# Where the early dense products are summed: in the stage that makes them, or later from DRAM

## The chip, the cores and the metric

The kernel runs on one core of a Trainium2 chip. The metric is device microseconds (us) of one execution of the whole program; a version's time is the median of its runs. The engines are TensorE (PE; PEld is its weight load), VectorE (DVE), ScalarE (ACT), GpSimd (POOL) and SyncE (SP). Here SP issues nearly all loads from DRAM, POOL issues nearly all stores.

## The reference

The output mixes two branches on x (2048 tokens, 640 columns), all float32: an FNet mixing y and a dense layer with Mish, weighted by a gate per token.

```python
g = sigmoid((x * gate_w).sum(-1, keepdims=True))
a = x @ wd_re.T ; b = x @ wd_im.T          # 640 x 640
y = c_re @ a - c_im @ b                    # 2048 x 2048
h = x @ w1 + b1                            # 640 -> 1728
act = h * tanh(softplus(h))                # Mish
out = g * y + (1 - g) * (act @ w2)         # 1728 -> 640
```

The kernel computes the same by first mixing over the sequence (u), then over the hidden columns (y).

## The kernel before, in words

Each float32 operand is split into a high and a low part (ACT copies the high part, DVE subtracts for the low part), and each product is three matmuls of 128x512: high by high, high by low, low by high (`mm3`). Products are arranged in a Strassen-like scheme of sums and differences of blocks, whose partial results leave PSUM into SBUF, return into a bank, or wait in DRAM. A tile `f` is a 128x512 buffer in SBUF (18 of them, pool `FS`), `x` a 128x640 buffer (6, pool `X`), `w` and `r` are split operands, `ps` are the 8 banks of PSUM.

The program is not issued as it is written. Every operation is first recorded in a graph (`Graph.add`). The order of the matmuls is the order in which the program writes them. For the other engines a planner (`Graph.run`) goes through the program with a cost for each operation: it gives each a wish time (`want`), sorts what is ready by it, hands out buffers of a pool only if enough are free for those that asked before (`granted`), and holds an operation back until its `since`; `by` pulls a wish time forward. What comes out is one fixed list of instructions for each engine. On the chip each engine takes its own list strictly in order and waits where an input or a buffer isn't ready.

The stages in order: products with the sequence matrices c_im and c_re (problems `sq`, tiles of x as weights, matrices c streamed from DRAM), wd's products (`hd`), the dense products of the later token groups (`dense_first`), and w2's products with the output (`ou`). A part of the dense products stands at the very front: for token groups t of 0 and 1 and the first six blocks f of w1, `early_first` makes the products of two of the five 128-column parts of x and stores them in DRAM as `early` (12 tiles, read again much later by `dense_first`, which the change leaves alone), and `early_second` makes those of the other three. Their steps (`unit`, three of each, in two `lines`) are spread between the steps of the first stage's problems 2, 3 and 0, so that their matmuls stand between those of c.

In `early_second` a step that has a result calls `end(c, t, f)`: it loads the `early` tile, DVE adds the new result to it (from PSUM in nine of twelve calls, `tt` at L314, and from SBUF in the other three), and `out_act` has ACT make the Mish (L624), and POOL store it as `act` (L306). Between two products in one bank the step also saves the bank to SBUF (`to_sbuf`, `f<-ps` at L323) and puts a saved value back into it (`copy`, `ps<-f`, L323), and the next matmul into that bank waits for this copy. The planner's order on ACT therefore decides how soon PE can go on.

Of the kernel before, what the change touches and what calls it, by code (L numbers as in the profile page):

```python
# [15 lines left out]
P = 128  # L16
# [11 lines left out]
DELAY, RATE = 2.2, 370e3  # L28
CALM, CALM_DMA, NEAR = 1.0, 3.0, 3.0
GATES = 130.0, 10.0  # L30
GATED = 600.0, 7.0


# [16 lines left out]
class Graph:  # L50
# [75 lines left out]
    def run(self, pools):  # L126

        self.wants()
        for op in self.ops:
            for v in op.vals:  # L130
                if v.pool and (v.ask is None or op.want < v.ask[0]):
                    v.ask = op.want, op.n, id(v)
        for op in self.ops:
            for v in op.vals:
                if v.pool and v.ask[1] == op.n:
                    also = [u.ask[0] for u in op.vals if u.pool is v.pool and u is not v]
                    if also:
                        v.ask = min(v.ask, (max(also), op.n, id(v)))
        for p in pools:
            p.asks = sorted({v.ask for op in self.ops for v in op.vals if v.pool is p})  # L140
            p.soon = sorted({v.ask for op in self.ops if op.prompt for v in op.vals if v.pool is p and v.ask[1] == op.n})
        missing = {op.n: len(op.deps) for op in self.ops}
        free = {e: 0.0 for e in ("PE", "ACT", "DVE", "SP", "POOL")}
        ready = {e: [] for e in free}
        pe = [op.n for op in self.ops if op.engine == "PE"][::-1]
        for op in self.ops:
            if not missing[op.n]:
                insort(ready[op.engine], (op.want, op.n))
        events, now, left, dma = [], 0.0, len(self.ops), 0.0
        waits = sorted({op.since for op in self.ops})  # L150

        def granted(op, blocked):
            for v in op.vals:
                if v.pool and v.t is None:
                    if v.pool in blocked:
                        return False
                    p, n = v.pool, bisect_left(v.pool.asks, v.ask)
                    if not op.prompt:
                        n += bisect_left(p.soon, (v.ask[0] + AHEAD,)) - bisect_left(p.soon, v.ask)
                    if len(p.free) <= n:  # L160
                        blocked.add(v.pool)
                        return False
            return True

        def bequeath(p):
            if p.heir and not p.asks:
                p.heir.free += [p.part(t) for t in p.free]
                p.free = []

        while left:  # L170
            began = False
            for e, line in ready.items():
                if free[e] > now + 1e-9 or not line:
                    continue
                if e == "PE":
                    i = next((i for i, x in enumerate(line) if x[1] == pe[-1]), None)
                    if i is not None and not granted(self.ops[pe[-1]], set()):
                        i = None
                else:
                    blocked = set()  # L180
                    i = next((i for i, x in enumerate(line)
                              if self.ops[x[1]].since <= now and granted(self.ops[x[1]], blocked)), None)
                if i is None:
                    continue
                op = self.ops[line.pop(i)[1]]
                if e == "PE":
                    pe.pop()
                for v in op.vals:
                    if v.pool and v.t is None:
                        v.pool.asks.remove(v.ask)  # L190
                        if v.ask in v.pool.soon:
                            v.pool.soon.remove(v.ask)
                        v.t = v.pool.free.pop(0)
                        bequeath(v.pool)
                op.emit()
                free[e] = now + op.hold
                if e in ("SP", "POOL"):
                    dma = max(now + DELAY, dma) + op.moves
                    end = dma + 0.1
                else:  # L200
                    end = now + op.took + 0.03
                heapq.heappush(events, (end, op.n, False))
                left -= 1
                began = True
            if began:
                continue
            times = [t for e, t in free.items() if t > now + 1e-9 and ready[e]]
            times += [t for t in waits if t > now][:1]
            if events:
                times.append(events[0][0])  # L210
            assert times, ("stuck", left, pe and self.ops[pe[-1]].at, [(p.name, len(p.free)) for p in pools])
            now = max(now, min(times))
            while events and events[0][0] <= now + 1e-9:
                _, n, held = heapq.heappop(events)
                op = self.ops[n]
                if held:
                    insort(ready[op.engine], (op.want, op.n))
                    continue
                for v in op.vals:
                    v.left -= 1  # L220
                    if not v.left and v.pool:
                        p = v.pool
                        p.free.append(v.t)
                        bequeath(p)
                for a in op.after:
                    missing[a.n] -= 1
                    if not missing[a.n]:
                        wait = min(CALM_DMA if op.engine in ("SP", "POOL") else CALM, a.want - now - NEAR)
                        if a.engine in ("ACT", "DVE") and wait > 0:
                            heapq.heappush(events, (now + wait, a.n, True))  # L230
                        else:
                            insort(ready[a.engine], (a.want, a.n))
# [8 lines left out]
def fnet_mish_gate(ctx: ExitStack, tc: tile.TileContext, xn, xt, c_re, c_im, wd_re, wd_im,  # L241
# [21 lines left out]
    def dram(name, rows=P, cols=N):  # L263
        return Val(t=dr.tile([rows, cols], F32, name=name))
# [33 lines left out]
        op.by, op.since = by, since  # L298
        return v

    def load_of(pool, d, rows=P):
        return load(pool, lambda: d.t, d, rows)

    def store(d, v, rows=P, queue=None):
        queue = queue or STORES
# [313 lines left out]
    def raw(t, k):  # L619
        return load(FS, xt[t, k])  # L620
# [80 lines left out]
        out_act(FC, t, a, a, FR, False)  # L701

    H = FP // 2
    early = {(t, f): dram(f"early{t}_{f}") for t in range(2) for f in range(FP)}

    def w1_twice(k0, fifth=False):

# [69 lines left out]
    def early_second():  # L777

        at, x = w1_twice(2, True), x_twice(2)
        d = [operand(raw(t, KD - 1), W) for t in range(2)]  # L780

        def unit(j):
            a, b = bank(), bank()

            def end(c, t, f):
                o = load_of(FS, early[t, f])
                tt(o, c, o, OP.add)
                out_act(f, t, o, o)
            mm3(a, at["b11", j], x["a11"], True, True)
            p = to_sbuf(a)  # L790
            yield
            mm3(b, at["t1", j], x["s1"], True, True)
            yield
            mm3(a, at["b21", j], x["a12"], False, False)
            mm3(a, at[("d", 0), j], d[0], False, True)
            end(a, 0, j)
            copy(a, p)
            yield
            mm3(a, at["t2", j], x["s2"], False, True)
            u = to_sbuf(a)  # L800
            yield
            mm3(a, at["t3", j], x["s3"], False, True)
            v = to_sbuf(a)
            tt(v, b, v, OP.add)
            yield
            mm3(b, at["b22", j], x["s4"], False, False)
            mm3(b, at[("d", 1), j], d[0], False, True)
            tt(u, b, u, OP.add)
            end(u, 0, j + H)
            yield  # L810
            mm3(a, at["t4", j], x["a22"], False, False)
            mm3(a, at[("d", 0), j], d[1], False, True)
            end(a, 1, j)
            yield
            copy(b, v)
            mm3(b, at[("d", 1), j], d[1], False, True)
            end(b, 1, j + H)
            yield
        kept.update(x, d=d)
        return [unit(j) for j in range(H)]  # L820
# [3 lines left out]
    def early_rests():  # L824
        for t, ks in ((0, ("a11", "a12")), (1, ("a21", "a22"))):
            dense_rest(t, [operand(raw(t, k)) for k in range(2)] + [kept[k] for k in ks] + [kept["d"][t]])

    def dense_first(tp):
        t1, t2 = tp, tp + 2
# [156 lines left out]
    for q in range(4):  # L986
        sq[q].second(seq.low)
        if q == 2:
            gates()
        sq[q].third()  # L990
    hd[0].first(hid.top)
    hd[1].first(hid.top)
    for p in hd:
# [58 lines left out]
```

## Time and profile before

| what | value |
|---|---|
| time, median of 3 runs (lowest, highest) | 865.77 us (864.66, 866.73) |
| profiled execution, whole | 866.31 us |
| its span, first to last instruction | 864.5 us |
| PE busy | 856.1 us, 3754 matmuls |
| DVE, ACT, POOL busy | 694.5, 486.9, 91.8 us |
| mean granted TensorE clock | 0.998 |
| moved by the DMA engines | 220.27 MB |

The span is 1.8 us shorter than the profiled execution's time; the rest lies around it. PE is busy in 99% of the span, so a time of this kernel is the number of matmuls by the distance of their starts, plus whatever time PE stands still or runs at a lower clock. Where PE has no gap, no other engine's work costs anything.

### The profile page before, as it was taken

Reading aid. Unit: us, or ns where it says so; the run is one execution under the profiler, and the core shown is the slowest. Engines: PE = TensorE matmul, PEld = TensorE weight load, DVE = VectorE, ACT = ScalarE, POOL = GpSimd, SP = SyncE. Lnnn points to the kernel's source line nnn. Section 1 sums busy time; section 2 is a strip of 40 time slices with the busy share of each in tenths; the row PEclk is TensorE's granted clock in tenths of the full one; section 3 lists DMA queues with packets and bytes.
Section 4 is the critical chain, followed back from the end, with each engine's and each line's share of the span. In section 5 each row is a group of like instructions: output and inputs, shape, how many; then the busy total and the mean of one; then the engine's idle time right before and its main releaser. Section 6 shows DMA issues by size and latency. Waiting matters only on the chain.

```text
span 864.5 us, 12193 instructions
## 1 busy us (share of the span) xinstructions
PE 856.1 (99%) x3754; PEld 704.8 (82%) x3754; DVE 694.5 (80%) x1241; ACT 486.9 (56%) x902; POOL 91.8 (11%) x167
## 2 busy tenths in 40 slices
PE   8999999999999999999999999999999999999998
PEld 6887788888888888888888888888888888888886
DVE  7978789986896778677999978997787996758493
ACT  6976776535354654456576733676566764533242
POOL 0122110002000200100020001022222100004000
PEclk9999999999999999999999999999999999999999
DMA  9888786777885957395778839678798876637943
GB/s 331 303 321 303 258 284 235 258 250 268 306 278 177 357 178 233 129 346 194 233 239 314 298 111 368 228 249 304 272 306 314 314 257 239 197 117 170 367 163 122
DMA packets 110946, 220.27 MB, mean 255 GB/s; under 512 B 13920, under 2 KB 18144, under 8 KB 110880
## 3 DMA queue, kind: packets, MB, share of 16 engines
q1 hardware_dynamic: 97184, 177.14, 60.0%
q0 software_dynamic: 13552, 42.22, 13.9%
q8 instruction: 29, 0.48, 0.2%
q14 instruction: 37, 0.30, 0.1%
q10 hardware_dynamic: 144, 0.13, 0.0%
HBM read 174.59 MB, written 44.84 MB: 254 GB/s over the span
## 4 chain that ended last, share of the span: by engine, by line
PE 97%; DMA 2%; DVE 0%; ACT 0%; issue 0%; SPq 0%; ACTq 0%; DVEq 0%
PE ps L350 97%; DMA x<-in_xn_dram 1%; DMA x<-in_w1a_dram 1%; DMA f<-in_c_im_dram 1%; SPq L296 0%; DVE f L314 0%; DVE x L314 0%; DVE r1l L345 0%; DVE r4l L345 0%; ACT r1h L344 0%; ACT ps L323 0%; ACT w19h L335 0%; ACT f L323 0%; DVE f L601 0%; ACT f L599 0%
## 5 line engine op out<-in xcount | busy, mean ns | idle before, releaser
L314 DVE TENSOR_TENSOR f<-f,f 128x512 f32<-128x512 f32 (+1 forms) x322 | 214.2, 683 | 5.1 <-DMA f<-act 2.0
L323 ACT ACTIVATE f<-ps 128x512 f32<-128x512 f32 x149 | 87.1, 595 | 63.4 <-PE ps L350 58.0
L314 DVE TENSOR_TENSOR f<-ps,f 128x512 f32<-128x512 f32 x101 | 66.9, 685 | 44.2 <-PE ps L350 34.2
L306 POOL DMA_DIRECT2D u<-f x40 | 21.6, 541 | 303.2 <-DVE f L314 289.8
L344 ACT ACTIVATE r9h<-f 128x512 fp32r<-128x512 f32 x40 | 25.3, 631 | 29.0 <-PE ps L350 20.5
L306 POOL DMA_DIRECT2D act<-f x52 | 28.1, 541 | 116.8 <-ACT f L624 74.1
L344 ACT ACTIVATE r5h<-f 128x512 fp32r<-128x512 f32 x38 | 24.0, 631 | 28.0 <-PE ps L350 22.2
L314 DVE TENSOR_TENSOR x<-x,x 128x256 f32<-128x256 f32 (+2 forms) x88 | 38.0, 445 | 2.2 <-DMA x<-in_xn_dram 1.5
L344 ACT ACTIVATE r1h<-f 128x512 fp32r<-128x512 f32 x39 | 24.5, 629 | 25.1 <-PE ps L350 19.6
L344 ACT ACTIVATE r4h<-f 128x512 fp32r<-128x512 f32 x38 | 23.9, 630 | 24.3 <-PE ps L350 18.7
L323 ACT ACTIVATE ps<-f 128x512 f32<-128x512 f32 x56 | 33.0, 598 | 8.2 <-DVE f L314 7.8
L344 ACT ACTIVATE r0h<-f 128x512 fp32r<-128x512 f32 x38 | 23.9, 629 | 23.8 <-PE ps L350 14.2
L344 ACT ACTIVATE r6h<-f 128x512 fp32r<-128x512 f32 x38 | 24.0, 631 | 23.2 <-PE ps L350 14.6
L344 ACT ACTIVATE r2h<-f 128x512 fp32r<-128x512 f32 x38 | 23.9, 629 | 22.8 <-PE ps L350 16.6
L344 ACT ACTIVATE r7h<-f 128x512 fp32r<-128x512 f32 x38 | 24.0, 631 | 21.5 <-PE ps L350 11.9
L345 DVE TENSOR_TENSOR r9l<-f,r9h 128x512 fp32r<-128x512 f32 x40 | 27.5, 686 | 10.5 <-ACT r9h L344 10.3
L344 ACT ACTIVATE r3h<-f 128x512 fp32r<-128x512 f32 x39 | 24.5, 628 | 19.9 <-PE ps L350 14.0
L344 ACT ACTIVATE r8h<-f 128x512 fp32r<-128x512 f32 x36 | 22.7, 630 | 21.2 <-PE ps L350 10.9
L345 DVE TENSOR_TENSOR r6l<-f,r6h 128x512 fp32r<-128x512 f32 x38 | 26.1, 686 | 10.4 <-ACT r6h L344 10.2
L345 DVE TENSOR_TENSOR r1l<-f,r1h 128x512 fp32r<-128x512 f32 x39 | 26.7, 686 | 9.0 <-ACT r1h L344 8.6
L624 ACT ACTIVATE f<-f,b1s 128x512 f32<-128x512 f32 x36 | 25.9, 718 | 14.1 <-DVE f L314 13.8
L345 DVE TENSOR_TENSOR r2l<-f,r2h 128x512 fp32r<-128x512 f32 x38 | 26.1, 688 | 9.5 <-ACT r2h L344 8.9
(2185 smaller groups left out, 2696.2 us busy)
## 6 DMA issues: line engine op xcount, KB each, us to landing
f<-in_c_im_dram SPq DMA_DIRECT2D x128, 256.0 KB, 4.7
f<-in_c_re_dram SPq DMA_DIRECT2D x128, 256.0 KB, 4.2
f<-act SPq DMA_DIRECT2D x84, 256.0 KB, 4.6
f<-u SPq DMA_DIRECT2D x80, 256.0 KB, 4.1
act<-f POOLq DMA_DIRECT2D x52, 256.0 KB, 4.0
f<-in_xt_dram SPq DMA_DIRECT2D x42, 256.0 KB, 4.3
u<-f POOLq DMA_DIRECT2D x40, 256.0 KB, 4.2
x<-in_xn_dram SPq DMA_DIRECT2D x24, 320.0 KB, 4.8
```

The lines of the kernel that those rows point to most:

```text
L306: dma(queue, lambda: ISSUE[queue].dma_start(d.t, v.t[:rows]), whole(v), whole(d), rows * N * 4)
L314: dve(lambda: nc.vector.tensor_tensor(o.t[rows, x], a.t[rows, y], b.t[rows, z], op=op), whole(a, b), whole(o), n)
L323: act(lambda: nc.scalar.activation(o.t, a.t, AF.Copy, scale=scale), whole(a), whole(o))
L344: act(lambda: nc.scalar.activation(r.t[0][:, :N], src.t[:, :N], AF.Copy), whole(src), [(r, 0)])
L345: dve(lambda: nc.vector.tensor_tensor(r.t[1][:, :N], src.t[:, :N], f32(r.t[0][:, :N]), op=OP.subtract), whole(src) + [(r, 0)], [(r, 1)])
L350: G.add("PE", lambda: nc.tensor.matmul(bank.t, w.t[wn][:, k * P:k * P + P], x.t[xn_][:, :N], start, stop, skip_group_check=True), [(w, (k, ...
L624: act(lambda: nc.scalar.activation(o.t[rows], src.t[rows], AF.Mish, **more), whole(src, table) + whole(b1s) * bias, whole(o), more=0.1)
```

## The change

`early_second` no longer loads the `early` tiles. Its twelve results are copied out of PSUM by ACT where they are in a bank (nine of them; three are already in SBUF) and stored by POOL in new DRAM tiles `late`. A new function `early_acts` loads each `early` tile with its `late` tile, adds the two on DVE, and then makes the Mish and the store as before. Its twelve sums are to begin, by the planner's clock, at 300 us and every 8 us after it. The planner also gets a second rule (`tight`) for the case that nothing can begin and no event is pending; then a result in PSUM may take a buffer that an earlier asker was waiting for.

```diff
+SUMS = 300.0, 8.0
...
                     p, n = v.pool, bisect_left(v.pool.asks, v.ask)
+                    if op.prompt and tight:
+                        n = bisect_left(p.soon, v.ask)
                     if not op.prompt:
...
+            if not times and not tight:
+                tight = True
+                continue
...
-            def end(c, t, f):
-                o = load_of(FS, early[t, f])
-                tt(o, c, o, OP.add)
-                out_act(f, t, o, o)
+            def end(o, t, f):
+                store(late[t, f], o)
...
-            end(a, 0, j)
+            end(to_sbuf(a), 0, j)
...
             end(u, 0, j + H)
...
-            end(a, 1, j)
+            end(to_sbuf(a), 1, j)
...
-            end(b, 1, j + H)
+            end(to_sbuf(b), 1, j + H)
...
+    def early_acts():
+
+        for i, key in enumerate(early):
+            since = SUMS[0] + SUMS[1] * i
+            o, v = (load_of(FS, d[key], since=since) for d in (early, late))
+            tt(o, o, v, OP.add)
+            G.ops[-1].by = since + SUMS[1]
+            out_act(key[1], key[0], o, o)
...
         sq[q].third()
+    early_acts()
     hd[0].first(hid.top)
```

The list of matmuls keeps its order (other buffers aside); the lists of the other engines move nearly everywhere, since the planner's choices follow from each other.

Place 1 is ACT's list in the second half of the early dense stage. The names: `w..h<-x` are high parts of weights from loads, `r..h<-f` high parts of streamed operands from loads, `f<-ps` is a save of a bank, `ps<-f` a value put back, `f<-f,b1s` a Mish. Before, from one value put back (`ps_70`) to the next (`ps_67`):

```order
L323 ACTIVATE ps_70<-f_100 128x512
L624 ACTIVATE f_109<-f_109,b1s 128x512
L335 ACTIVATE w2h<-x_115 128x256
L335 ACTIVATE w16h<-x_115 128x128
L323 ACTIVATE f_100<-ps_70 128x512
L344 ACTIVATE r2h<-f_96 128x512
L335 ACTIVATE w15h<-x_112 128x640
L344 ACTIVATE r0h<-f_99 128x512
L335 ACTIVATE w19h<-x_113 128x640
L323 ACTIVATE ps_67<-f_95 128x512
```

And now, between the same two:

```order
L331 ACTIVATE ps_70<-f_100 128x512
L343 ACTIVATE w18h<-x_112 128x128
L352 ACTIVATE r9h<-f_104 128x512
L331 ACTIVATE f_102<-ps_70 128x512
L343 ACTIVATE w17h<-x_116 128x640
L343 ACTIVATE w21h<-x_111 128x640
L331 ACTIVATE f_100<-ps_67 128x512
L331 ACTIVATE ps_67<-f_93 128x512
L352 ACTIVATE r7h<-f_103 128x512
L331 ACTIVATE f_109<-ps_70 128x512
L352 ACTIVATE r0h<-f_110 128x512
```

The Mish is gone, a save of `ps_67` has come in ahead of its return, and the two copies `r7h` and `r0h` from loads, one of which stood ahead of the value put back, stand behind it.

Place 2 is SP's list of loads at the same place. Before:

```order
L296 DMA f_96<-in_c_re_dram 128x512
L296 DMA f_103<-early_4_300 128x512
L296 DMA f_99<-in_xt_dram 128x512
L296 DMA x_113<-in_w1a_dram 128x640
L296 DMA f_106<-early_2_298 128x512
L296 DMA x_111<-in_xn_dram 128x640
L296 DMA f_93<-in_xt_dram 128x512
L296 DMA f_96<-early_5_295 128x512
L296 DMA f_109<-in_xt_dram 128x512
```

And now:

```order
L304 DMA f_104<-in_xt_dram 128x512
L304 DMA f_108<-in_c_re_dram 128x512
L304 DMA f_98<-in_c_re_dram 128x512
L304 DMA f_96<-in_c_re_dram 128x512
L304 DMA f_103<-in_xt_dram 128x512
L304 DMA f_97<-in_c_re_dram 128x512
L304 DMA f_110<-in_xt_dram 128x512
L304 DMA x_112<-in_w1b_dram 128x320
L304 DMA x_115<-in_xn_dram 128x512
L304 DMA x_116<-in_xn_dram 128x640
L304 DMA x_111<-in_w1a_dram 128x640
```

Before, the two x tiles (`in_xt`) and the block of w1 (`in_w1a`) for the copies of place 1 stood between loads of `early`; now no load of `early` is there, and the x tiles stand four to ten rows ahead of the block of w1.

Place 3 is SP's list in the course of the last two problems of the first stage. Before:

```order
L296 DMA f_110<-in_c_re_dram 128x512
L296 DMA f_96<-in_c_im_dram 128x512
L296 DMA f_100<-in_c_im_dram 128x512
L296 DMA f_101<-in_c_im_dram 128x512
L296 DMA f_97<-ps_319 128x512
```

And now:

```order
L304 DMA f_98<-in_c_im_dram 128x512
L304 DMA f_106<-in_c_im_dram 128x512
L304 DMA f_97<-early_0_296 128x512
L304 DMA f_102<-late_0_308 128x512
L304 DMA f_103<-ps_331 128x512
```

Two loads of one sum have come in between the streamed ones; eleven more such pairs stand in this part of the list, all of them ahead of the first load of `in_wd_im`.

More of the change, by code (lines that the diff above doesn't have):

```diff
@@ L168, in bequeath @@
                 p.free = []
+        tight = False
         while left:
@@ L205, in run @@
             if began:
+                tight = False
                 continue
@@ L299, in load, with load_of @@
         return v
-    def load_of(pool, d, rows=P):
-        return load(pool, lambda: d.t, d, rows)
+    def load_of(pool, d, rows=P, since=0.0):
+        return load(pool, lambda: d.t, d, rows, since=since)
     def store(d, v, rows=P, queue=None):
@@ L703, in fnet_mish_gate @@
     H = FP // 2
-    early = {(t, f): dram(f"early{t}_{f}") for t in range(2) for f in range(FP)}
+    early, late = ({(t, f): dram(f"{n}{t}_{f}") for t in range(2) for f in range(FP)} for n in ("early", "late"))
     def w1_twice(k0, fifth=False):
```

## The prediction

> **What bounds the kernel now.** First the head and the busy times of the page:
>
> ```profile
> span 864.5 us, 12193 instructions
> PE 856.1 (99%) x3754; PEld 704.8 (82%) x3754; DVE 694.5 (80%) x1241; ACT 486.9 (56%) x902; POOL 91.8 (11%) x167
> ```
>
> PE is the bound. The change adds no matmul and takes none away, so only time in which PE stands still or runs below its clock can be won or lost. The view of waits, asked for PE alone, has one row that matters (the others lie in the first 8 us, where the loads change by one swapped pair):
>
> ```profile
> PE ps L350 <- ACT ps L323: 2.4, 2, 1.9
> ```
>
> Two waits, both for a value that ACT puts back into a bank. PE's own timeline shows where they are, and what they cost (start, duration, ..., idle before and its releaser):
>
> ```profile
> 85.12 0.39 PE L350 MATMUL ps<-r0h,w1l 128*128 128x512 f32 x1
> 86.03 0.50 PE L350 MATMUL ps<-r6h,w25h 128*128 128x512 f32 x1 [0.52 <-ACT ps L323]
> ...
> 86.60 0.40 PE L350 MATMUL ps<-r6h,w25l 128*128 128x512 f32 x1
> ...
> 88.68 0.39 PE L350 MATMUL ps<-r8h,w2l 128*128 128x512 f32 x1
> ...
> 90.72 0.39 PE L350 MATMUL ps<-r1h,w25l 128*128 128x512 f32 x1
> 92.96 0.50 PE L350 MATMUL ps<-r6h,w25h 128*128 128x512 f32 x1 [1.85 <-ACT ps L323]
> ...
> 94.25 0.63 PE L350 MATMUL ps<-r7l,w3h 128*128 128x512 f32 x1
> ...
> 96.38 0.63 PE L350 MATMUL ps<-r7h,w3h 128*128 128x512 f32 x1
> ...
> 97.42 0.39 PE L350 MATMUL ps<-r5h,w22h 128*128 128x512 f32 x1
> ```
>
> The undisturbed step is read between the two holes: 88.68 to 90.72 is 9 steps, 2.04 / 9 = 0.2267 us. Hole 1, 85.12 to 86.60, is 3 steps: 1.48 - 0.68 = 0.80 lost. From 86.60 to 90.72 are 18 steps: 4.12 - 4.08 = 0.04. Hole 2, 90.72 to 97.42, is 13 steps: 6.70 - 2.95 = 3.75. Only about 2.0 of that is standing still; behind it the steps are 0.43 (94.25 to 96.38, 5 steps in 2.13), nearly double. The granted clock says why (window: length, busy times and counts of PE, PEld, DVE, ACT, POOL, then clock, DMA share, GB/s):
>
> ```profile
> 85.35:86.03 0.68, 0.16 (x1) 0.00 (x0) 0.68 (x3) 0.65 (x2) 0.00 (x0) 1.00 0.92 349
> 90.95:92.96 2.01, 0.16 (x1) 0.00 (x0) 1.46 (x3) 1.80 (x4) 0.00 (x0) 1.00 1.03 405
> 92.96:97.42 4.46, 4.46 (x12) 3.51 (x13) 3.21 (x7) 2.82 (x5) 0.54 (x1) 0.62 0.76 285
> ```
>
> After the hole of 2.01 us the mean clock was 0.62; the hole of 0.68 had no such sequel. The holes together cost 0.80 + 0.04 + 3.75 = 4.59 us.
>
> Why ACT was late, in ACT's timeline, and for hole 1 in DVE's:
>
> ```profile
> 85.38 0.60 ACT L323 ACTIVATE ps<-f 128x512 f32<-128x512 f32 x1 [2.08 <-DVE f L314]
> ...
> 90.84 0.63 ACT L344 ACTIVATE r0h<-f 128x512 fp32r<-128x512 f32 x1 [1.48 <-DMA f<-in_xt_dram]
> 91.68 0.74 ACT L335 ACTIVATE w19h<-x 128x640 fp32r<-128x640 f32 x1 [0.21 <-DMA x<-in_w1a_dram]
> 92.33 0.58 ACT L323 ACTIVATE ps<-f 128x512 f32<-128x512 f32 x1
> ```
>
> ```profile
> 83.11 0.42 DVE L314 TENSOR_TENSOR x<-x,x 128x256 f32<-128x256 f32 x1 [1.48 <-DMA x<-in_xn_dram]
> ...
> 84.66 0.68 DVE L314 TENSOR_TENSOR f<-ps,f 128x512 f32<-128x512 f32 x1
> ```
>
> Hole 1: DVE waited 1.48 for a load, so the sum in `end`, which must read the bank (84.66), was late, and ACT could not overwrite that bank before. Hole 2: ACT took its list in order, stood behind the late copy of an x tile (`r0h`, 1.48) and of a block of w1 (0.21), and reached the value for PE only at 92.33. Both come from loads that land late. SP's waits from 60 to 110 us and the landing times from 60 to 100 us say why these are late:
>
> ```profile
> SPq L296 <- DMA act<-f: 8.0, 4, 3.1
> SPq L296 <- DMA ps<-f: 6.3, 3, 5.4
> SPq L296 <- DMA early<-f: 4.3, 2, 2.6
> ```
>
> ```profile
> f<-early SPq DMA_DIRECT2D x7, 256.0 KB, 5.0
> ...
> ps<-f POOLq DMA_DIRECT2D x3, 256.0 KB, 7.0
> ...
> x<-in_w1a_dram SPq DMA_DIRECT2D x1, 320.0 KB, 5.3
> ```
>
> SP stands 18.6 us in these three rows for stores to land, since only then is an `f` buffer free for its next load; all later loads stand behind it. The `early` loads are seven of those that ask for such buffers here.
>
> **The change, part by part.** The durations come from the page's groups:
>
> ```profile
> L314 DVE TENSOR_TENSOR f<-f,f 128x512 f32<-128x512 f32 (+1 forms) x322 | 214.2, 683 | 5.1 <-DMA f<-act 2.0
> L323 ACT ACTIVATE f<-ps 128x512 f32<-128x512 f32 x149 | 87.1, 595 | 63.4 <-PE ps L350 58.0
> ...
> L306 POOL DMA_DIRECT2D act<-f x52 | 28.1, 541 | 116.8 <-ACT f L624 74.1
> ...
> L624 ACT ACTIVATE f<-f,b1s 128x512 f32<-128x512 f32 x36 | 25.9, 718 | 14.1 <-DVE f L314 13.8
> ```
>
> *Early stage, removed.* Twelve loads (256 KB each; at the 405 GB/s of the window row 0.65 us, together 7.8 us of transfers), twelve sums on DVE (8.2 us) and twelve Mish on ACT (12 x 0.718 = 8.6 us). *Added:* nine copies out of PSUM (9 x 0.595 = 5.4 us of ACT). The twelve stores stay, to another place, at POOL's 0.541 each. None of this is on PE's path by itself; what counts is the two holes. At hole 1 the bank is now emptied by ACT itself, just ahead of the value put back (place 1 of the order), so the wait of DVE for its load no longer stands between. At hole 2 one of the two copies from loads (`r0h`) now stands behind the value put back, and the x tiles are asked for much earlier, with no `early` load between (place 2). I take both holes as gone: -4.59 us. Bounds: 0 (they stay) and -4.59.
>
> What is late next there is the block of w1: its copy (`w21h`) still stands ahead of the value put back, and its load 18 matmuls ahead of that copy, by the step 4.1 us. The value put back has a reserve of about 1.2 us more, so a landing of 5.3, the row above, just uses all up. I take 0, bound +0.6.
>
> *New tight spots.* ACT's nine copies must come between a product's end and the next value in the bank. Two places have less room than before:
>
> ```profile
> 34.05 1.12 ACT L323 ACTIVATE ps<-f 128x512 f32<-128x512 f32 x2
> ```
>
> ```profile
> 35.03 0.39 PE L350 MATMUL ps<-r3h,w10h 128*128 128x512 f32 x1
> ```
>
> ```profile
> 40.88 0.69 DVE L314 TENSOR_TENSOR f<-ps,f 128x512 f32<-128x512 f32 x1 [0.21 <-ACT f L323]
> ```
>
> ```profile
> 41.83 0.39 PE L350 MATMUL ps<-r8h,w14h 128*128 128x512 f32 x1
> ```
>
> At 35.03 the first of the two values had arrived at about 34.05 + 0.56 = 34.61, 0.4 ahead; one more copy of 0.595 in front, if nothing else gives way, makes it 0.2 late. At 41.83 the bank had been read at 41.57, 0.26 ahead; a copy by ACT in place of DVE's sum may be earlier or later. I take 0 for both, since ACT loses the Mish in front of it, with bounds 0 and +0.6 each. A hole that short had no sequel in the clock (window 85.35:86.03).
>
> *Later stage, added.* By place 3 the twelve pairs of loads stand among the last loads of c_im, ahead of wd's stage: some 1270 to 1710 matmuls stand ahead of them, which by the step puts them at about 296 to 396 us. The stage there (windows, then landing times from 320 to 420 us):
>
> ```profile
> 300.00:400.00 100.00, 100.00 (x443) 82.80 (x442) 74.08 (x117) 46.35 (x78) 5.37 (x10) 1.00 0.63 217
> ```
>
> ```profile
> 360.00:380.00 20.00, 20.00 (x90) 16.57 (x89) 14.44 (x23) 12.44 (x22) 5.37 (x10) 1.00 0.84 310
> ```
>
> ```profile
> f<-in_c_im_dram SPq DMA_DIRECT2D x56, 256.0 KB, 4.5
> f<-in_c_re_dram SPq DMA_DIRECT2D x12, 256.0 KB, 2.7
> ```
>
> DVE: 74.1 + 8.2 = 82.3 of 100 us; ACT 46.4 + 8.6 = 55; POOL 5.4 + 12 x 0.541 = 11.9. DMA: 24 loads and 12 stores by 0.65 are 23.4 us on a share of 0.63, so 0.86, like the 0.84 of 360 to 380 us, in which PE has no gap. New wait: a sum stands in DVE's list behind its two loads, and behind it the low parts of c; its Mish likewise on ACT. The pairs are asked for some 22 or more matmuls (5 us) ahead, and loads land here after 2.7 to 4.5. I take 0; bounds 0 and two holes of 3.75 each, +7.5.
>
> *Sum*, against the profiled execution's 866.31: 866.31 - 4.59 = 861.72. That execution is 0.54 above the median of 865.77; I don't take this off, since the holes hang on landing times and are probably what scatters. If it is taken off, 861.2.
>
> **The rivals.** What a measurement of this kernel can tell is about 0.2%, 1.7 us: same is 864.0 to 867.5.
>
> *A, small holes.* The in-order ACT list still stands behind a late load (block of w1 at about 89 us), or the copies at 35 and 42 us come late. For it: the reserves of 0.2 to 1.2 us above. Against: the transfers of that stage fall by 7.8 us. Price 0.6 for one of the three bounds to 1.8 for all, so 862.3 to 863.5, about 863.0.
>
> *B, the holes stay or move.* SP is still held by stores (18.6 us in three rows; `late` stores replace `act` stores one for one), some load is late, and one hole like hole 2 stands somewhere in the first 120 us: 861.7 + 3.75 = 865.5. Against: with twelve loads fewer, twelve buffers fewer are asked for.
>
> *C, the slow clock isn't the hole's.* Of hole 2, steps from 92.96 to 97.42 (12, 4.46 against 2.72) cost 1.74. If these come from something periodic, they stay: 861.7 + 1.7 = 863.4. The rows speak against it: the clock is 1.00 in every other window shown.
> The Trainium skill, "TensorE: Matmul & The Clock Gate", "Why this matters for your kernels", would let the clock fall only after idle gaps of more than about 3 us, and by that a hole of 2.01 us would not be the cause. Here the drop followed directly on the hole, so the trace differs from that figure; no run yet shows the stretch without the hole.
>
> *D, slower: SP blocked at 300 to 396 us.* Twenty-four loads more ask for `f` buffers that come free only when a store has landed, up to 5.4 us each in the row on `ps<-f`, and twelve new `act` stores are such. If a wait of that length delays a load of c beyond its lead, PE stops as in hole 2. One such hole gives back 3.75 (865.5, no difference); it becomes slower from 5.8 us of new loss on, so from two: 861.7 + 7.5 = 869.2. For it: DMA at 0.86 in that stage, within the 0.76 to 1.03 of the three windows at the holes. Against: the loads of c run well ahead, and 360 to 380 us, at 0.84, has no gap.
>
> That the sums are not where the change's words put them (wd's stage) is certain by place 3 and alters nothing in the sum.
>
> **How the numbers follow.** Forecast 0.67 (861.7), A 0.13 (863.0), C 0.03 (863.4), B 0.07 (865.5), D 0.10 (869.2). Faster: 0.67 + 0.13 + 0.03 = 0.83; same 0.07; slower 0.10. The range: low end 861.2 less half a microsecond for the scatter of a median (861.2 is the sum from the median), 860.7; high end over A and C to 864.0, which leaves out B and D (0.17).
>
> **What would show it.** Right: in the trace after, PE has no wait for `ps<-f` between 80 and 100 us, clock 1.00 there, step 0.2267 throughout; DMA share in 300 to 400 us about 0.86 with no PE gap; span about 859.9. Wrong: a PE gap with a clock below 1.00 behind it near 35, 42 or 89 us (A, B), slow steps without a gap (C), or SP waiting for `act<-f` and PE for a copy of c between 296 and 396 us (D).

## The result, and the profile after

The changed kernel takes 861.81 us (median of 6 runs, 861.61 to 862.09) against 865.25 (6 runs, 863.77 to 866.73) for the kernel before: ratio 0.9959, 95% interval 0.9946 to 0.9972. Its profiled execution took 861.99 us. The page's head, and all that PE waits for:

```profile
span 860.2 us, 12275 instructions
PE 854.5 (99%) x3754; PEld 704.8 (82%) x3754; DVE 693.2 (81%) x1241; ACT 491.8 (57%) x911; POOL 98.3 (11%) x179
```

```profile
PE ps L920 <- PEq L1056: 0.8, 1, 0.8
PE ps L358 <- DVE r0h L350: 0.3, 1, 0.3
PE ps L358 <- DVE r1l L353: 0.2, 1, 0.2
```

All three lie in the first 8.4 us; after that the view shows no wait of PE. At the place of hole 2 the value put back is there 0.91 us before its matmul (ACT's, then PE's timeline):

```profile
88.12 0.59 ACT L331 ACTIVATE f<-ps 128x512 f32<-128x512 f32 x1
88.75 0.60 ACT L331 ACTIVATE ps<-f 128x512 f32<-128x512 f32 x1
```

```profile
90.26 0.39 PE L358 MATMUL ps<-r0h,w24h 128*128 128x512 f32 x1
```

Both stages by windows (length, busy times of PE, PEld, DVE, ACT, POOL, clock, DMA share, GB/s):

```profile
80.00:100.00 20.00, 20.00 (x89) 16.54 (x89) 14.51 (x30) 15.63 (x31) 2.38 (x5) 1.00 0.50 167
...
300.00:400.00 100.00, 100.00 (x443) 82.84 (x442) 74.48 (x121) 53.74 (x93) 11.84 (x22) 1.00 0.84 292
```

The waits of SP from 60 to 110 us and the landings from 60 to 100 us: the longest wait for a store is now 3.0 us, and the stores of saved banks and the block of w1 land sooner (7.0 and 5.3 before):

```profile
SPq L304 <- DVE w12l L344: 8.9, 2, 8.7
...
SPq L304 <- DMA early<-f: 3.1, 2, 1.6
SPq L304 <- DMA late<-f: 3.0, 1, 3.0
```

```profile
ps<-f POOLq DMA_DIRECT2D x3, 256.0 KB, 3.4
x<-in_w1a_dram SPq DMA_DIRECT2D x1, 320.0 KB, 2.9
```

The x tiles (`in_xt`) land no sooner, after 4.1 us against 4.0. They and the block of w1 are asked for earlier, as SP's timeline shows, before the change and after it:

```profile
78.17 0.38 SPq L296 DMA_DIRECT2D x<-in_xn_dram  x1
78.64 0.40 SPq L296 DMA_DIRECT2D f<-early  x1
84.51 0.33 SPq L296 DMA_DIRECT2D f<-in_c_re_dram  x1
...
85.86 0.33 SPq L296 DMA_DIRECT2D f<-in_xt_dram  x1
86.28 0.38 SPq L296 DMA_DIRECT2D x<-in_w1a_dram  x1
```

```profile
71.94 0.33 SPq L304 DMA_DIRECT2D f<-in_xt_dram  x1
...
83.54 0.33 SPq L304 DMA_DIRECT2D x<-in_w1a_dram  x1
```

The x tile asked for at 71.94 is the one that `r0h` copies. SP also stands still in the changed kernel, even longer than before: 8.7 us, until 83.54, for a buffer that `w12l` still reads. PE loses nothing by it, since the x tile was asked for ahead of that wait and the block of w1 still comes in time.

The ends of the ledger are the last matmul before and after:

```profile
860.29 0.39 PE L350 MATMUL ps<-w0h,w22l 128*128 128x512 f32 x1
```

```profile
855.56 0.39 PE L358 MATMUL ps<-w0h,w23l 128*128 128x512 f32 x1
```

PE ends 4.73 us sooner: 4.59 from the two holes, 0.22 from a small one before the change (below), 0.11 lost in the start (third matmul of the second operand at 8.38 instead of 8.27). What follows the last matmul is about 0.4 longer (860.2 - 855.56 = 4.64, against 4.21). The small one is here (PE's timeline before):

```profile
609.92 0.39 PE L350 MATMUL ps<-r2h,w19l 128*128 128x512 f32 x1
610.25 0.50 PE L350 MATMUL ps<-w12h,w18h 128*128 128x512 f32 x1
610.59 0.40 PE L350 MATMUL ps<-w12l,w18h 128*128 128x512 f32 x1
```

Two steps of 0.33 and 0.34 there; in the kernel after none is longer than 0.24 at that time.

### The profile page after: what moved, and what is told of

Its sections match the earlier page's. It is cut to its first block, busy times and chain, and to the rows that moved or that the text cites. A ratio compares the mean times of both kernels' runs of the same rounds, so it can differ in the third digit from the quotient of the medians.

```text
span 860.2 us, 12275 instructions
## 1 busy us (share of the span) xinstructions
PE 854.5 (99%) x3754; PEld 704.8 (82%) x3754; DVE 693.2 (81%) x1241; ACT 491.8 (57%) x911; POOL 98.3 (11%) x179
## 4 chain that ended last, share of the span: by engine, by line
PE 99%; DMA 1%; SPq 0%; DVE 0%; ACT 0%; issue 0%; ACTq 0%
PE ps L358 99%; DMA f<-in_c_im_dram 1%; SPq L304 0%; DVE r1l L353 0%; ACT r1h L352 0%; DVE f L609 0%; ACT f L607 0%; ACTq L607 0%
## 5 line engine op out<-in xcount | busy, mean ns | idle before, releaser
L322 DVE TENSOR_TENSOR f<-f,f 128x512 f32<-128x512 f32 x331 | 220.4, 686 | 6.4 <-DMA f<-act 2.3
L331 ACT ACTIVATE f<-ps 128x512 f32<-128x512 f32 x158 | 92.6, 596 | 67.6 <-PE ps L358 61.6
L322 DVE TENSOR_TENSOR f<-ps,f 128x512 f32<-128x512 f32 x92 | 60.9, 687 | 40.9 <-PE ps L358 39.7
L353 DVE TENSOR_TENSOR r5l<-f,r5h 128x512 fp32r<-128x512 f32 x39 | 26.9, 689 | 12.1 <-ACT r5h L352 11.9
L352 ACT ACTIVATE r8h<-f 128x512 fp32r<-128x512 f32 x37 | 23.3, 629 | 20.1 <-PE ps L358 11.8
L353 DVE TENSOR_TENSOR r8l<-f,r8h 128x512 fp32r<-128x512 f32 x37 | 25.5, 689 | 9.1 <-ACT r8h L352 8.8
```

What stands on the lines that cost most here:

```text
L322: dve(lambda: nc.vector.tensor_tensor(o.t[rows, x], a.t[rows, y], b.t[rows, z], op=op), whole(a, b), whole(o), n)
L331: act(lambda: nc.scalar.activation(o.t, a.t, AF.Copy, scale=scale), whole(a), whole(o))
L352: act(lambda: nc.scalar.activation(r.t[0][:, :N], src.t[:, :N], AF.Copy), whole(src), [(r, 0)])
L353: dve(lambda: nc.vector.tensor_tensor(r.t[1][:, :N], src.t[:, :N], f32(r.t[0][:, :N]), op=OP.subtract), whole(src) + [(r, 0)], [(r, 1)])
```

## The experiments

The question: which part closes the holes, the order on ACT and DVE, the transfers, or SP's wait for stores? And is the later place of the sums free? Ratios are against the kernel before, run beside them on the same chip.

**One list reordered (b_act, b_dve, b_both).** Rows of the lists of before, moved in the order of issue:

```diff
 ACT  w15h<-x_112
+ACT  ps_67<-f_95
 ACT  r0h<-f_99
 ACT  w19h<-x_113
-ACT  ps_67<-f_95
...
+DVE  f_109<-ps_70,f_109
 DVE  x_115<-x_112,x_114
 DVE  r4l<-f_103,r4h
 DVE  f_110<-f_110,f_98
-DVE  f_109<-ps_70,f_109
```

> The kernel before; on ACT alone, the value put back into the bank stands ahead of the two copies from loads (r0h, w19h) at about 91 us. All loads, stores and sums stay. If hole 2 is ACT's list standing behind late loads, and those loads are needed by nobody soon, hole 2 goes with its slow clock and hole 1 stays: 3.75 us less than before, about 861.5 against its median of 865.3. If the late loads themselves are what PE lacks, the hole only moves behind the next matmul that needs them: 865 or more.

> The kernel before; on DVE alone, the sum that reads the bank (84.66 us) stands ahead of the three operations that wait for, or stand behind, a load of x. If hole 1 is DVE's list standing behind that load, hole 1 (0.80 us) goes, and hole 2 stays: about 864.5. If the bank is not what ACT waited for, no difference. A later hole 2 may also grow by what PE arrives earlier, since it hangs on a landing: then no gain at all, about 865.3.

> The kernel before with both of these moves, nothing else: the early sums stay in the early stage, no late tiles. If the two holes are all that the change won, about 861.8, the same as the changed kernel, without its 6.3 MB of further traffic. If the change wins by fewer transfers in the early stage, about 865.

Measured: b_act 864.01 (0.9980, 0.9972 to 0.9989), b_dve 864.64 (0.9986, 0.9977 to 0.9995), b_both 863.67 (0.9981, 0.9972 to 0.9990). None came to 861.8. These three moves change part of the computation: in b_act the value put back also overtakes the sum that reads the bank, in b_dve and b_both the sum overtakes the last six matmuls into its bank. PE then waited for that sum (b_both, PE's timeline):

```profile
82.62 0.50 PE L356 MATMUL ps<-w20h,w15h 128*128 128x512 f32 x1 [1.13 <-DVE f L320]
```

So b_dve and b_both say nothing on hole 1. That b_dve came out near its 864.5 is luck: hole 1 is gone there, but this new wait (1.11) stands in its place, and hole 2 is 0.94. b_act still says something: hole 2 is gone, a wait of 0.48 stands at 100.44 us instead, and hole 1 is 1.37 in its profile instead of 0.52, with the same DVE list as before. The holes' size varies from execution to execution.

**The same with the meaning kept (b_act2, b_both2).** The value put back goes behind the sum that reads its bank; the sum of hole 1 stays behind its matmuls, and two sums that stood ahead of it go behind it:

```diff
 DVE  f_107<-ps_67,f_107
+ACT  ps_67<-f_95
+ACT  r0h<-f_99
...
-DVE  x_115<-x_112,x_114
-DVE  f_110<-f_110,f_98
 DVE  f_109<-ps_70,f_109
+DVE  x_115<-x_112,x_114
+DVE  f_110<-f_110,f_98
```

> The kernel before; on ACT alone the value put back into the bank stands right behind the sum that reads that bank, ahead of the two copies from loads (r0h, w19h). Every operation keeps its meaning, all loads, stores and sums stay. If hole 2 is ACT's list behind late loads, it goes: at most 3.75 us less, with hole 1 (0.8 in the profile before, 1.6 in that of b_act) left: 862.0 to 863.5. If the loads themselves are lacking, a hole comes up at the next matmul that needs one, as at 100.4 us in b_act: 864 or more.

> As b_act2, and on DVE the sum that reads the bank at 84.66 us stands ahead of the sum of x tiles that waits for a load, and of one more sum. If two orders are all that the change won, no gap is left between 80 and 100 us and the time is within 0.5 of the changed kernel, 861.8 to 862.3, with the early sums still in the early stage. If late loads come through elsewhere, one gap of 0.5 to 1.5 us stays: 862.5 to 863.5.

Measured: 863.94 (0.9987, 0.9977 to 0.9997) and 864.16 (0.9993, 0.9984 to 1.0003). The first lies between its two ranges, the second above both of its own. Where the waits went (PE's timeline of b_act2, then of b_both2):

```profile
91.06 0.50 PE L357 MATMUL ps<-r6h,w25h 128*128 128x512 f32 x1 [0.44 <-ACT ps L330]
...
94.61 0.50 PE L357 MATMUL ps<-r5h,w22h 128*128 128x512 f32 x1 [0.54 <-DVE f L321]
```

```profile
92.69 0.50 PE L357 MATMUL ps<-r6h,w25h 128*128 128x512 f32 x1 [2.05 <-ACT ps L330]
```

and why, in ACT's timeline and in SP's waits (60 to 100 us) of b_both2:

```profile
88.52 0.42 ACT L342 ACTIVATE w2h<-x 128x256 fp32r<-128x256 f32 x1 [3.58 <-DVE x L321]
```

```profile
SPq L303 <- DMA ps<-f: 5.6, 1, 5.6
```

SP again issues nothing from 79.5 to 85.5. With the two copies out of the way, ACT stands instead at `w2h`, behind a DVE sum of x tiles that had itself waited for loads, and the hole is back. (b_both2 has a second wait of 0.54, at 96.24.) These orders are worth 0.6 to 1.1 us by the ratios; the late loads come through at the next operation that needs one.

**Fewer bytes, same lists (b_tiny, b_ps).** Twelve early loads, or three stores of saved banks and their later loads, move 16 of 512 columns and leave out the rest, so the sums made from them are not the kernel's:

```diff
 o = load_of(FS, early[t, f])
+G.ops[-1].emit = lambda: nc.sync.dma_start(o.t[:, :16], early[t, f].t[:, :16])
...
-dma_start(d.t, v.t[:rows])
+dma_start(d.t[:, :16], v.t[:rows, :16])    # for ps3 alone
```

> The kernel before, every list in its order, but the twelve early loads of the second half fetch 16 of 512 columns (the sums are then made with what else is in the buffer). If the loads were late because these transfers take their time on the DMA engines, the loads at 86 us land about 1 us earlier and hole 2 shrinks below 1 us: about 862 to 863. If they were late because SP stood still for buffers whose stores had not landed (5.4 us at once before 84.5), their issue at 85.9 and 86.3 stays and so does most of hole 2: 864.5 to 865.3.

> The kernel before, every list in its order, but the three stores of saved banks at 78 to 80 us (and their later loads) move 16 of 512 columns. If hole 1 and hole 2 hang on the one wait of SP, 5.4 us for the first of these stores to land, SP goes on some 3 us or more earlier, the loads for both holes are early, and 861.8 to 862.5 comes out, with every early load still there. If the crowded DMA engines as such made the loads late (0.75 MB less is little), 864 to 865.

Measured: b_tiny 863.73 (0.9984, 0.9972 to 0.9996), b_ps 863.47 (0.9977, 0.9966 to 0.9989). PE's one gap between 20 and 600 us in each, and SP's wait for the stores in b_ps (60 to 110 us):

```profile
91.18 0.50 PE L353 MATMUL ps<-r6h,w25h 128*128 128x512 f32 x1 [1.11 <-ACT ps L326]
```

```profile
91.55 0.50 PE L353 MATMUL ps<-r6h,w25h 128*128 128x512 f32 x1 [0.53 <-ACT ps L326]
```

```profile
SPq L299 <- DMA ps<-f: 4.3, 2, 3.3
```

In both hole 1 is gone and hole 2 is short, with no slow clock. Neither expectation held: both times lie between the two ranges. Fewer bytes in either place are worth 1.4 to 2.0 us by the ratios, so neither is the whole. They don't separate the transfers from SP's wait, though. In b_tiny the block of w1 was asked for at 85.92, hardly sooner than the 86.28 before, but landed after 3.9 us instead of 5.3. In b_ps SP's longest wait for these stores fell from 5.4 to 3.3, not to nothing, for even with 8 KB they landed after 5.1 us (7.0 with 256 KB); the block of w1 was asked for at 86.03, in an execution that runs 0.7 us later from its start, and landed after 4.2.

**The old order on the changed kernel (a_undo).**

```diff
 ACT  f_100<-ps_67
+ACT  r7h<-f_103
+ACT  r0h<-f_110
 ACT  ps_67<-f_93
-ACT  r7h<-f_103
 ACT  f_109<-ps_70
-ACT  r0h<-f_110
```

> The changed kernel; on ACT the copies r7h and r0h from loads stand again ahead of the value put back at 90 us, as before the change. The value has 0.9 us in hand there and two copies take 1.04. If the order won the time, a gap of up to 0.3 us and more where a load is late: 862.1 to 864. If it was the earlier loads, these have landed, PE loses 0 to 0.3 us: 861.8 to 862.1.

Measured: 862.64 (0.9974, 0.9965 to 0.9983); the changed kernel, run beside others, had 0.9959. PE's gap is at another matmul (PE, then ACT):

```profile
89.80 0.50 PE L364 MATMUL ps<-r7h,w2l 128*128 128x512 f32 x1 [0.49 <-ACT r7h L358]
```

```profile
89.11 0.63 ACT L358 ACTIVATE r7h<-f 128x512 fp32r<-128x512 f32 x1 [0.61 <-PE ps L364]
89.65 0.61 ACT L358 ACTIVATE r0h<-f 128x512 fp32r<-128x512 f32 x1
```

The move let `r7h` overtake the last matmul that reads its buffer, which changes that product and makes PE wait for the copy: this 0.5 is the experiment's own. What it does show is that neither copy waits for a load any more, where `r0h` waited 1.48 before.

**The sums at other times (a_460, a_dense, a_early).**

```diff
-SUMS = 300.0, 8.0
+SUMS = 460.0, 8.0    # a_460; a_dense: 300.0, 2.0; a_early: 60.0, 5.0
```

> The changed kernel with the sums from 460 us on instead of 300, so really in the course of wd's stage (460 to 555 us). If the later place is free wherever loads lead by some 5 us, as in 300 to 396 us, no gap: 861.8. If the fuller stage (DVE 19.6 of 20 us at 460 to 480 us before) has no room for 8.2 us of sums, gaps: 862.5 to 866.

> The changed kernel with the sums every 2 us instead of every 8, so all 36 added transfers (23.4 us of transfer time) fall into 288 to 330 us, beside 0.62 to 0.69 of that stage's own. That is rival D's condition forced: DMA asked for more than 1.0 of 42 us. If buffers and DMA decide, c's loads come late and PE loses one or two times 3.75 or small gaps: 863 to 869. If c's loads lead by enough, 861.8 to 862.2.

> The changed kernel with the sums from 60 us on, every 5: both halves go through DRAM, and the twelve early loads, twelve late loads and the stores all lie between 60 and 130 us, so 24 transfers more than before in the stage with the holes. If what the change won is that the stage's loads don't wait for buffers and stores, it is lost, and more: 865 to 870. If the nine copies in place of sums that read the bank, and the new order, are what won, it stays near 862 to 863.

Measured: a_460 866.77 (1.0016, 1.0007 to 1.0026), a_dense 865.46 (0.9996, 0.9986 to 1.0005), a_early 904.89 (1.0456, 1.0435 to 1.0477). In a_460, where the sums lie in wd's stage, the early stage keeps its gain, but PE has gaps later. The two longest, and the window of that stage in it and in the changed kernel:

```profile
523.05 0.50 PE L358 MATMUL ps<-r4h,w10h 128*128 128x512 f32 x1 [1.07 <-ACT ps L331]
...
627.97 0.50 PE L358 MATMUL ps<-w11h,w15h 128*128 128x512 f32 x1 [1.55 <-DVE f L322]
```

```profile
460.00:555.00 95.00, 93.35 (x408) 76.07 (x407) 81.41 (x145) 55.02 (x105) 12.89 (x24) 1.00 0.89 314
```

```profile
460.00:555.00 95.00, 95.00 (x421) 78.69 (x420) 86.26 (x158) 55.83 (x109) 6.97 (x13) 1.00 0.76 262
```

The time is just above the expected 862.5 to 866. The second gap lies 73 us behind that window, and no run shows why.

In a_dense c's streamed tiles come late, one after the other (PE; then the landing of c's loads from 300 to 340 us, 2.7 in the kernel before and 3.5 in the changed one):

```profile
330.62 0.51 PE L358 MATMUL ps<-r3h,w11h 128*128 128x512 f32 x1 [0.25 <-ACT r3h L352]
...
333.22 0.50 PE L358 MATMUL ps<-r0h,w17h 128*128 128x512 f32 x1 [0.45 <-ACT r0h L352]
```

```profile
f<-in_c_re_dram SPq DMA_DIRECT2D x23, 256.0 KB, 6.0
```

Three such places cost 3.5 us together. In a_early the largest gap hangs on loads by a detour: `r2h` stands in ACT's list behind a step of the gates, for which ACT waits 13.95 us until 179 us, and behind eleven Mish; and DVE's products for the gates wait for their loads of x, the last of them 2.88 us (PE, then DVE):

```profile
188.92 0.79 PE L358 MATMUL ps<-r2h,w12h 128*128 128x512 f32 x1 [19.02 <-ACT r2h L352]
```

```profile
178.15 0.82 DVE L942 SCALAR_TENSOR_TENSOR x<-x,x 128x640 f32<-128x640 f32 x1 [2.88 <-DMA x<-in_xn_dram]
```

SP had stood still for stores of `late` before that (its waits from 60 to 140 us):

```profile
SPq L304 <- DMA late<-f: 26.8, 9, 4.9
```

That speaks for the first of the two theories, loads that wait for buffers and stores. But the time lies far outside both ranges, and the gates, which neither theory had in it, make the largest single gap; so a_early shows only that this time for the sums is far worse.

**Holes of known length (clock).**

```diff
+HOLES = {398: 17, 517: 19, 817: 29, 881: 37}
...
+for _ in range(op.slow):
+    nc.scalar.activation(idle, a.t[:, :P], AF.Copy)
 nc.scalar.activation(o.t, a.t, AF.Copy, scale=scale)
```

> The changed kernel with 17, 19, 29 and 37 small idle copies of 128 columns (about 0.2 us each) on ACT ahead of four values put back, far apart (about 366, 466, 711 and 812 us); results unused. By the time in hand PE should stand still there for about 1.0, 1.4, 2.0 and 2.8 us. If standing still for 2 us lowers the clock, as read from hole 2, steps of 0.43 follow the last two and not the first two, each costing some 1.8 us more: about 861.8 + 7.2 + 3.6 = 872.6. If hole 2 and its slow clock fell together by chance, or only more than 3 us lower it, no slow steps: 869.0.

Measured: 893.43 (2 runs). The small copies took 0.34 us apiece, not 0.2 (5.77 / 17), so all four holes came out longer than planned, 3.15, 3.79, 7.44 and 7.71 us (ACT; then PE at the first two):

```profile
365.69 5.77 ACT L345 ACTIVATE idle<-f 128x128 f32<-128x128 f32 x17
```

```profile
372.00 0.50 PE L374 MATMUL ps<-r7h,w13h 128*128 128x512 f32 x1 [3.15 <-ACT ps L346]
...
373.31 0.63 PE L374 MATMUL ps<-r7h,w18l 128*128 128x512 f32 x1
...
376.68 0.40 PE L374 MATMUL ps<-r0l,w13h 128*128 128x512 f32 x1
...
478.35 0.50 PE L374 MATMUL ps<-r5h,w1h 128*128 128x512 f32 x1 [3.79 <-ACT ps L346]
```

A stretch of slow steps follows each: 3.37 us after the first (373.31 to 376.68), like the 3.4 us after hole 2, and some 6 and 4 us after the two longest. The point between 1 and 3 us that it was to find, it missed.

## Why the prediction was right

- **The two holes as the whole of the gain** (861.72 from 866.31): right in place and size. Both are gone, and the sum is 0.09 from the median and 0.27 from the profiled execution. The 0.22 at 610 us and the 0.11 of the start were not in it, nor the 0.4 behind the last matmul; that they nearly cancel is luck.
- **Not taking off the 0.54 between execution and median**, since the holes scatter: borne out. The spread of the runs fell from 2.96 us to 0.48, and b_act's hole 1 was 1.37 where the profile of before had 0.52. It also means that 4.59 is what that execution lost; the medians differ by 3.44. Part of the scatter is the slow clock: of the 88 executions of the kernel before that ran beside the experiments, 36 had a mean granted clock of 0.998 or less, which is what one slow stretch of 3.4 us makes of it, and their medians are 866.4 to 866.6 us, against 864.5 to 864.8 for the rest. In each experiment that edits the kernel before, at most two of its 11 or 12 executions had such a clock, so a part of what it gained on the median is that the slow stretch came seldom.
- **Why hole 1 closes.** The prediction laid it to DVE's wait for a load, which the runs bear out, and that load's lateness to SP's waits for stores and to slow landings; of these two only the second holds. The load of `in_xn` in question was asked for at 78.17 us at the latest, before SP stood still (78.64 to 84.51). From that request to DVE's start it took 5.7 us in b_act (hole 1: 1.37) and 4.9 in the kernel before (0.52); with 4.4 in b_act2, at most 3.9 in b_tiny and 3.8 in b_ps there is no hole 1, all with DVE's list unchanged. In the changed kernel the sum that stood behind that load is gone from this place altogether.
- **Why hole 2 closes.** The text named two reasons: `r0h` behind the value put back, and earlier loads. Both are there in the trace after, and the runs give bounds for their weight: by the ratios, order alone with the meaning kept gave 0.6 to 1.1 us (b_both2, b_act2; the first not clear of zero), shorter transfers or stores alone 1.4 to 2.0 (b_tiny, b_ps), the change 3.5. SP's longest wait for a store of a saved bank was 4.2 to 5.7 us in every version that keeps the early loads in place and the stores whole. It isn't harmful by its length, as the 8.7 us of the changed kernel show, but by what stands behind it.
- **What it was not.** The Mish that left ACT's list did not delay the two values: ahead of both, ACT had stood idle (2.08 and 1.48 us). The planner's second rule (`tight`) is never used when the changed kernel is planned.
- **Tight spots at 35 and 42 us, rivals A and B**: no gap. The block of w1 was asked for 2.7 us sooner and landed after 2.9 us, not 5.3.
- **Later stage**: DMA 0.84 (0.86 worked out), ACT 53.7 (55), POOL 11.8 (11.9). DVE was mis-sized: 74.5 instead of 82.3, since the lists moved and only four more operations fall into that window; it changed nothing.
- **Rival D** was a real mechanism that did not come to decide: SP waited for act stores (296 to 396 us), for which it had no wait there before,

```profile
SPq L304 <- DVE f L322: 17.3, 21, 6.6
SPq L304 <- DMA act<-f: 15.2, 7, 3.6
```

and PE lost nothing there. That c's loads lead by enough is our reading of it, and a_dense fits: with the sums every 2 us, c's loads come late and all of the gain is given back. At 460 us (a_460) the kernel is slower than before, by 0.16%. So the result rests on the place and the spacing of the sums.
- **Rival C**: wrong here; without the hole there are no slow steps.

What stays open is the share of each cause beyond these bounds: no run leaves out SP's wait entirely while keeping the early loads.

## What to carry to other kernels

Where one engine issues all loads in a fixed order, look at what that queue waited for before a hole, and at which loads stand behind the wait; its length alone says little. An engine's list can be reordered around a late load, but in b_both2 the next load behind the same wait took its place. Moving work to a later stage pays only if that stage's streamed loads lead by more than the moved transfers delay them; here the same sums were free at one every 8 us, cost all the gain at one every 2, and made the kernel slower 160 us later. Where holes hang on landings and the runs scatter, one profile is one draw: here it lost 4.59 us by its holes, while the medians differ by 3.44.

## What the runs showed of the hardware

Whether a wait of PE lowers the clock is not set by its length alone. Waits of 1.11, 1.13, 1.37 and 2.05 us (b_tiny, b_both, b_act, b_both2) left the steps at 0.23, and so did waits of 1.83 and 2.98 in a_early. The wait of 1.85 in the profile before was followed by 3.4 us of steps of 0.43, and so were one of 1.87 in a_early and those of 3.15 and 3.79 in the run with holes of known length.

What fits all of these is a fixed beat. In a_early the clock falls at 125.09, 172.88 and 503.97 us, which is 14 and 97 times 3.413 us apart, and 3.41 is also the length of the shortest slow stretches. The wait of 1.87 (501.76 to 503.63) lies inside one such beat, while the 2.98 (133.98 to 136.96) lies across the border of two; of b_both2, where the beat is counted back from the clock's fall behind the last matmul (862.35), 1.7 of the 2.05 lie in one (windows: length, PE's busy time, ..., clock, DMA share, GB/s; the last row is of b_both2):

```profile
500.56:503.97 3.41, 1.54 (x8) 0.95 (x6) 3.41 (x11) 1.30 (x4) 0.10 (x1) 1.00 0.30 96
503.97:507.38 3.41, 3.41 (x10) 2.64 (x9) 1.64 (x4) 1.92 (x5) 1.51 (x3) 0.50 0.69 185
135.33:138.74 3.41, 1.78 (x8) 1.48 (x9) 3.41 (x6) 2.30 (x4) 0.55 (x1) 1.00 0.92 289
```

```profile
90.93:94.34 3.41, 1.65 (x7) 1.40 (x8) 2.19 (x4) 2.68 (x6) 0.00 (x0) 1.00 0.98 377
```

In the traces of this case, each set on its own beat, the clock fell after every beat at full clock in which PE was busy for 1.56 us or less (eight, with that of hole 2, which ends at 93.71, as the highest), and after none with 1.65 or more. So whether hole 2 was followed by the slow clock was a matter of where it fell on the beat, and that the profiled execution had it is chance. The Trainium skill, "TensorE: Matmul & The Clock Gate", "What's actually happening", has a free-running window of about 3.4 us decide on the clock; the length of the slow stretches and the beat agree with it. The figure of the Trainium skill, "TensorE: Matmul & The Clock Gate", "Why this matters for your kernels", by which gaps up to about 3 us are harmless, does not hold here, by the 1.85 and the 1.87.
